# A retention-plus-MLP kernel: the first eight steps written as single operations, in another order on every engine and in the load queue

## The chip, the cores and the metric

One core of one Trainium2 chip runs the whole kernel. The metric is device time in microseconds (us). The kernel before was run nine times: median 701.33 us, 700.83 to 703.13. One of its executions was profiled; that one took 701.53 us by the same clock, and its profile spans 699.7 us, so 1.83 us lie around the span.

## What is computed

```python
# q, k, v: (B, H, S, D) = (4, 8, 768, 64); w_in (512, 2048), w_out (2048, 512); inputs float64
state = zeros((B, H, D, D))
for t in range(S):
    state = gamma * state + k[:, :, t] (outer) v[:, :, t]      # gamma: one number per head
    y[:, :, t] = q[:, :, t] @ state / sqrt(D)
x = y as (B*S, H*D) = (3072, 512)
h = x @ w_in
out = (h - tanh(h)) @ w_out                                    # (3072, 512)
```

q, k and v reach the kernel as float32; w_in and w_out arrive as 64-bit words, and the kernel turns them into float32 itself.

## The kernel before, in words

**Attention.** The 3072 tokens are 24 chunks of 128. For a chunk ci the kernel loads k, q and v (128 x 512 each, `load_chunk`, L230), multiplies q and v by powers of gamma (`scale`, L248), and, for the chunks of the start, turns k and q by four TensorE transposes each (`turn`, L264, matmuls of L276), copied out of PSUM by ScalarE (`turn_copy`, L282). `products` (L314) makes k-v products (L325) and k-q scores (L331). On VectorE `mask` (L335) masks the scores and `state` (L343) adds the chunk to the running state in two operations (L348 or L350, then L354). `outputs` and `outputs_rest` (L379) make y, `see` (L409) is four tiny ScalarE copies on which the second half of the outputs waits, and `keep_x` (L425) copies y into x.

**Weights.** There are 32 weight tiles of 512 KB. Tile W0 to W3 are four column blocks of w_in, W4 to W7 four row blocks of w_out, W8 to W11 columns of w_in again, and so on. A tile of w_in is three DMAs (L159), one of w_out is one (L154). Turning one into float32 is two ScalarE operations (`convert_begin`, L177 and L178), four VectorE operations (`convert_bits`, L186 to L192) and two more, a multiply and an add (`convert_end`, L200 and L204), on GpSimd or VectorE.

**MLP.** A step is 256 tokens by 256 columns of the hidden layer. `up` (L444) makes one half (128 columns) with eight matmul instructions; h lies in one of two PSUM banks. ScalarE then makes u = h*h, tanh(h), two polynomial factors q0 and q1 and the flag `large` (L454 to L472). VectorE does five operations (L482, L486, L495, L502, L503) that end in g. `down` (L511) multiplies g by w_out into the o banks; `add_up` sums o over the runs of steps. Steps 0 and 1 are the first 256 tokens by the first and second 256 columns (weights W0, W1 and W2, W3 going up; W4, W5 and W6, W7 going down), steps 2 and 3 the same for the next 256 tokens, and so on up to step 7. Steps 8 and 9 use W8 to W11 going up.

**Order.** The program is scheduled by hand: every engine runs its instructions in the order of the Python calls, each engine strictly in its own order, and so do the DMAs of the SyncE queue. The order of the first eight steps (`BEGUN = 8`), with chunks 0 to 7 and weights W0 to W11 in them, is a string of pieces, L850 to L859, each a letter and a number. In the kernel before a piece is often several operations:

| piece | what it does | engine |
|---|---|---|
| L, W | load a chunk's k, q, v; load a weight tile | SyncE queue |
| s, w | scale q; scale v | VectorE or GpSimd, by fixed sets (`SCALED`, L806) |
| t, T, c, C | turn k, turn q; copy each out | TensorE; ScalarE |
| p, m, z | products; mask; both state operations | TensorE; VectorE |
| b, e, r, y | outputs, see, rest of the outputs, keep x | TensorE, ScalarE |
| A, D, G | the three parts of a weight's conversion (2, 4 and 2 operations) | ScalarE; VectorE; GpSimd, or VectorE for W0 and W1 (`ENDED`, L807) |
| u, v | the two halves of `up` for a step | TensorE |
| a, q, d, g | u and tanh; three ScalarE factors; first two, last three VectorE operations of a step | ScalarE, VectorE |
| o, E | both `down` products of a step; both sums | TensorE; ScalarE or VectorE |
| x | the next TensorE piece is preceded by so many filler matmuls (`keep_busy`, L215, matmuls of L217, two instructions each) | TensorE |

The filler counts of the kernel before are x8, x4, x5, x3, x3, x5, x7, x2. Buffers that the order has to live with: k and q have two, v four, the raw words of weights three (plus six early places that are later the x tiles), `head`, `low` and `power` two each, q0 and q1 one each, u, tanh, `large` and h two each. After the string a loop runs the other steps (from step 8 on), two steps behind with the `down` products; it begins with W12 and W13, and chunk 8.

Of the kernel before, what the change touches and what calls it, by code (L numbers as in the profile page):

```python
# [16 lines left out]
P = 128  # L17
# [14 lines left out]
def kernel(  # L32
# [137 lines left out]
    def convert_begin(i):  # L170
        if i not in raws:
            return
        raw = raws.pop(i).rearrange("p (n two) -> p two n", two=2)
        lo, hi = raw[:, 0], raw[:, 1]
        head = stage.tile([P, BANK], U32, tag="head", name=f"head_{i}")
        low = stage.tile([P, BANK], F32, tag="low", name=f"low_{i}")
        nc.scalar.activation(head.bitcast(F32), hi.bitcast(F32), AF.Abs)  # L177
        nc.scalar.activation(low, lo, AF.Copy, scale=2.0 ** -52)  # L178
        words[i] = [hi, head, low]

    def convert_bits(i):
        if i not in words:
            return
        hi, head, low = words[i]
        power = stage.tile([P, BANK], U32, tag="power", name=f"power_{i}")
        nc.vector.tensor_scalar(head.bitcast(F32), head.bitcast(F32), HI_MIN, HI_MAX,  # L186
                                op0=ALU.max, op1=ALU.min)
        nc.vector.tensor_scalar(head, head, 3, 0x3FFFFFF8, op0=ALU.logical_shift_left,
                                op1=ALU.bitwise_and)
        nc.vector.scalar_tensor_tensor(head, in0=hi, scalar=0xC0000000, in1=head,  # L190
                                       op0=ALU.bitwise_and, op1=ALU.bitwise_or)
        nc.vector.tensor_scalar(power, head, 0xFF800000, None, op0=ALU.bitwise_and)  # L192
        words[i] = [head, low, power]

    def convert_end(i, engine):
        if i not in words:
            return
        dst, src = weight_ends(i)
        head, low, power = words.pop(i)
        engine.tensor_tensor(low, low, power.bitcast(F32), op=ALU.mult)  # L200
        head = head.bitcast(F32)
        if isinstance(src, list):
            low, head = (t.rearrange("p (c n) -> p c n", c=NC) for t in (low, head))
        engine.tensor_tensor(dst, low, head, op=ALU.add)  # L204

    def convert(i):
        convert_begin(i)
        convert_bits(i)
        convert_end(i, nc.gpsimd)
# [20 lines left out]
    def load_chunk(ci):  # L230
        if ci >= NCH:
            return
        b, j = divmod(ci, CPB)
        loaded[ci] = []
        for nm, src in (("k", k), ("q", q), ("v", v)):
            t = inp.tile([P, H, D], F32, tag=nm, name=f"{nm}_{ci}", bufs=4 if nm == "v" else 2)
            rows = src[b, :, ts(j, P), :]
            if nm == "q" and ci < WIDE:
                for i in range(2):
                    nc.sync.dma_start(  # L240
                        out=t[:, ts(i, RUN)].rearrange("p r d -> p (r d)"),
                        in_=rows[i::2].rearrange("g (p r) d -> p g (r d)", r=RUN),
                    )
            else:
                nc.sync.dma_start(out=t, in_=rows.rearrange("h p d -> p h d"))
            loaded[ci].append(t)

    def scale(ci, which, engine):  # L248
# [4 lines left out]
        if which == 0 and ci < WIDE:  # L253
            if not wide:
                wide.append(mid.tile([P, 2, RUN, 2, D], F32, tag="apart", name="wide", bufs=1))
            out_ = loaded[ci][1] = wide[0][:, ci % 2]
# [7 lines left out]
    def turn(ci, which, early=False):  # L264

        if early:
            tp = bank("o", f"kqTp{which}_{ci}")
        else:
            if which == 0:
                turned[ci] = banks("t", f"kqTp_{ci}")  # L270
            tp = turned[ci][:, which]
# [5 lines left out]
        if early:  # L277
            turned.setdefault(ci, []).append(tp)
# [3 lines left out]
    def turn_copy(ci, which=None):  # L282
        if ci not in sides:
            sides[ci] = mid.tile([P, 2, NP, P], F32, tag="kqT", name=f"kqT_{ci}")
        side = sides[ci]
        for i in range(2) if which is None else (which,):
            tp = turned[ci][:, i] if which is None else turned[ci][i]
            if i:
                nc.scalar.copy(out=side[:, 1].rearrange("p n (t r) -> p n t r", r=RUN),
                               in_=tp.rearrange("p (r t n) -> p n t r", r=RUN, n=NP))  # L290
            else:
                nc.scalar.copy(out=side[:, 0], in_=tp.rearrange("p (n t) -> p n t", n=NP))
# [21 lines left out]
    def products(ci):  # L314

        kh, _, vh = loaded[ci]
# [26 lines left out]
    def state(ci):  # L343
        halves = scores[ci]
        j = ci % CPB
        if j == 0:
            states[ci] = mid.tile([P, 2, NP, D], F32, tag="state", name=f"state_{ci}", bufs=3)
            nc.vector.tensor_copy(states[ci][:, 1], halves[:, 0, 1])  # L348
        else:
            nc.vector.tensor_tensor(states[ci][:, 1], halves[:, 0, 1], states[ci][:, 0],  # L350
                                    op=ALU.add)
        if j < CPB - 1:
# [10 lines left out]
    def outputs(ci):  # L363
# [5 lines left out]
        a_, st = masked.pop(ci), states.pop(ci)  # L369
# [59 lines left out]
    gT = {}  # L429
# [7 lines left out]
    def up(n, m2, i):  # L437

        if (n, m2) not in hps:
            hps[n, m2] = bank("h", f"h_{n}_{m2}")  # L440
        hp = hps[n, m2][:, ts(i, TH)]
        keep_busy(hp[:, :P])
        for c in range(NC):
            nc.tensor.matmul(hp, w1[:, c, ts(2 * m2 + i, P)], xT[n // 2][:, c, ts(n % 2, TH)],  # L444
                             start=(i == 0 and c == 0), stop=(c == NC - 1),
# [358 lines left out]
    EARLY_TURNS = 4  # L804

    SCALED = {2, 4, 5}, {0, 1, 2}  # L806
    ENDED = {0, 1}  # L807

    def engine(i, among):
        return nc.vector if i in among else nc.gpsimd  # L810

    def begin_h(s):

        hps[steps[s][:2]] = bank("h", "h_early")
        keep_busy(hps[steps[s][:2]][:, :P])

    pieces = {
        "L": load_chunk,
        "W": load_weights,
        "s": lambda c: scale(c, 0, engine(c, SCALED[0])),  # L820
        "w": lambda c: scale(c, 1, engine(c, SCALED[1])),
        "t": lambda c: turn(c, 0, c < EARLY_TURNS),
        "T": lambda c: turn(c, 1, c < EARLY_TURNS),
        "c": lambda c: turn_copy(c, 0),
        "C": lambda c: turn_copy(c, 1 if c < EARLY_TURNS else None),
        "p": products,
        "m": mask,
        "z": state,
# [4 lines left out]
        "A": convert_begin,  # L833
        "D": convert_bits,
        "G": lambda i: convert_end(i, engine(i, ENDED)),
        "u": lambda s: up(*steps[s][:2], 0),
        "v": lambda s: up(*steps[s][:2], 1),
        "a": lambda s: shrink_begin(*steps[s][:2]),
        "q": lambda s: shrink_factors(*steps[s][:2]),
        "d": lambda s: shrink_multiply(*steps[s][:2]),  # L840
        "g": lambda s: [f(*steps[s][:2]) for f in (shrink_last_factor, shrink_end)],
        "o": lambda s: [down(*steps[s][:2], j, *steps[s][2:]) for j in range(2)],
        "E": lambda s: [add_up(*steps[s][:2], j) for j in range(2)],
        "h": begin_h,
        "k": lambda s: keep_busy(hps[steps[s][:2]][:, :P]),
# [5 lines left out]
    L0 L1 x8 t0 c0 W0 s0 x4 T0 w0 W1 C0 p0 t1 m0 c1 s1 z0 b0 w1 T1 e0 C1 p1 L2 z1 r0 A0 m1  # L851
    W2 D0 y0 x5 h0 b1 A1 G0 t2 x3 k0 c2 e1 s2 L3 r1 x3 k0 D1 T2 y1 C2 u0 w2 A2 G1 p2 t3 m2 v0 c3 L4 z2
# [205 lines left out]
```

## Time and profile before

| | |
|---|---|
| median of nine runs | 701.33 us |
| the profiled execution | 701.53 us, span 699.7 us |
| busy, share of the span | TensorE 99%, VectorE 74%, ScalarE 62%, GpSimd 51% |
| first eight steps on TensorE, by the timeline | from the first transposes at 4.63 us to the end of step 5's down products at 91.90 us |
| VectorE busy from 0 to 92 us | 70.45 us |
| DMA over the first 58 us | 12.6 MB by the SyncE queue |

Times within the profile count from the start of the span. A row of the timeline reads: start, length, engine, line, operation, output <- input, shape, count, and in brackets the idle time ahead of it with what ended it. A row of the chain of waits reads: start, length, engine and line that the end of the program can be followed back to. "PE" is TensorE's matmuls, DVE is VectorE, ACT is ScalarE, POOL is GpSimd, SP is SyncE.

### The profile page before, as it was taken

To read this page: it belongs to the slowest core of one execution; us is meant where nothing else is said; L and a number is where in the kernel's file an instruction comes from. 1 tells how busy PE (TensorE), PEld (TensorE's weight loads), DVE (VectorE), ACT (ScalarE), POOL (GpSimd) and SP (SyncE) were. 2 spreads that over 40 slices of the span, in tenths; PEclk is the share of its full clock that TensorE was granted. 3 is DMA by queue.
4 is the path that set the end of the run, shared out by engine and by line. 5 is a ranking of instruction groups with operands and counts; after the bars stand their busy time and mean duration, and the time that the engine had idled before them with its cause. 6 is when DMAs were issued, how large, how long until landed. Compare 5 with 4: busy or idle time off the path is not lost.

```text
span 699.7 us, 16645 instructions
## 1 busy us (share of the span) xinstructions
PE 691.7 (99%) x6602; PEld 580.5 (83%) x6602; DVE 519.8 (74%) x888; ACT 432.6 (62%) x818; POOL 356.2 (51%) x523
## 2 busy tenths in 40 slices
PE   8999999999999999999999999999999999999997
PEld 7786666676767667789999999999999999999996
DVE  4898889989898865677776686677686676766765
ACT  4577677676866755565555665555665555566553
POOL 1364445554454686878854453354443444544333
PEclk9999999999999999999999999999999999999999
DMA  8790439978778666500000000000000000000001
GB/s 228 212 276 24 135 107 218 214 202 223 190 210 212 180 166 171 161 34 2 0 1 16 16 1 30 2 1 31 2 1 31 1 1 31 0 17 16 1 16 47
DMA packets 119678, 59.97 MB, mean 86 GB/s; under 512 B 101808, under 2 KB 112688, under 8 KB 119600
## 3 DMA queue, kind: packets, MB, share of 16 engines
q1 hardware_dynamic: 117008, 50.21, 28.1%
q10 hardware_dynamic: 2592, 8.69, 3.3%
q8 instruction: 52, 0.85, 0.5%
q14 instruction: 26, 0.21, 0.1%
HBM read 35.83 MB, written 14.68 MB: 72 GB/s over the span
## 4 chain that ended last, share of the span: by engine, by line
PE 92%; DVE 3%; DMA 2%; ACT 1%; issue 1%; POOL 0%; POOLq 0%; DVEq 0%; ACTq 0%
PE h L758 28%; PE o L511 15%; PE h L444 14%; PE fast_t L649 10%; PE y L649 8%; PE fast_o L649 8%; PE y L379 3%; PE s L331 2%; PE s L325 1%; PE kqTp L276 1%; DMA kqT<-rows 1%; PE h_early L444 1%; DMA rows<-apart 1%; PE kqTp L217 1%; PE h_early L217 1%
## 5 line engine op out<-in xcount | busy, mean ns | idle before, releaser
L600 POOL TENSOR_TENSOR s<-g 128x128 f32<-128x128 f32 x64 | 29.3, 458 | 190.5 <-DVE g L503 186.6
L457 ACT ACTIVATE th<-h 128x512 f32<-128x512 f32 x64 | 38.2, 598 | 142.4 <-DVE h L775 139.9
L511 PE MATMUL o<-w,g 128*128 128x512 f32 x256 | 115.9, 595 | 0.0
L444 PE MATMUL h<-xT,w 128*128 128x256 f32 x480 | 110.2, 382 | 0.0
L444 PEld LDWEIGHTS h<-xT,w 128*128 128x128 f32 x480 | 90.1, 190 | 20.6 <-issue 8.9
L503 DVE COPY_PREDICATED g<-large,th 128x512 f32<-128x512 int32 x96 | 81.7, 851 | 9.7
L511 PEld LDWEIGHTS o<-w,g 128*128 128x128 f32 x256 | 47.6, 190 | 47.4 <-issue 44.5
L758 PEld LDWEIGHTS h<-xT,w 128*128 128x128 f32 x512 | 76.8, 191 | 8.4 <-ACT fast_head L763 1.0
L482 DVE TENSOR_TENSOR th<-h,th 128x512 f32<-128x512 f32 x94 | 64.2, 683 | 21.3 <-ACT th L455 20.0
L773 DVE TENSOR_TENSOR h<-h,fast_head 128x256 f32<-128x256 f32 x64 | 27.7, 432 | 68.7 <-PE h L758 63.3
L758 PE MATMUL h<-xT,w 128*128 128x128 f32 x512 | 78.3, 275 | 0.2 <-ACT fast_head L763 0.2
L200 POOL TENSOR_TENSOR low<-low,power 128x512 f32<-128x512 f32 x30 | 39.6, 1321 | 63.1 <-DVE power L192 53.6
L495 DVE SCALAR_TENSOR_TENSOR g<-q,h 128x512 f32<-128x512 f32 x64 | 44.0, 688 | 36.1 <-ACT q L471 34.8
L463 ACT ACTIVATE q<-u,tab 128x512 f32<-128x512 f32 x96 | 69.7, 726 | 1.8
L471 ACT ACTIVATE q<-u,tab 128x512 f32<-128x512 f32 x96 | 69.5, 723 | 0.0
L472 ACT ACTIVATE large<-u,tab 128x512 f32<-128x512 f32 x96 | 68.5, 713 | 0.0
L758 PE MATMUL h<-x,w 128*128 128x128 f32 x448 | 68.3, 275 | 0.0
L486 DVE SCALAR_TENSOR_TENSOR h<-q,h 128x512 f32<-128x512 f32 x94 | 64.9, 691 | 3.7 <-ACT q L463 3.7
L758 PEld LDWEIGHTS h<-x,w 128*128 128x128 f32 x448 | 59.0, 192 | 0.0
L763 ACT COPY fast_head<-h 128x512 f32<-128x512 f32 x64 | 37.5, 585 | 19.2 <-PE h L758 19.1
L502 DVE TENSOR_TENSOR g<-g,u 128x512 f32<-128x512 f32 x64 | 47.5, 742 | 0.0
L768 POOL TENSOR_TENSOR fast_head<-fast_head 128x256 f32<-128x256 f32 x64 | 46.9, 732 | 1.0 <-ACT fast_head L763 1.0
(195 smaller groups left out, 1487.8 us busy)
## 6 DMA issues: line engine op xcount, KB each, us to landing
rows<-apart ACTq DMA_DIRECT2D x16, 512.0 KB, 4.4
k<-in_k_dram SPq DMA_DIRECT2D x24, 256.0 KB, 3.8
v<-in_v_dram SPq DMA_DIRECT2D x24, 256.0 KB, 5.2
raw<-in_moe_w_out_dram SPq DMA_DIRECT2D x12, 512.0 KB, 4.2
out_dram<-sum SPq DMA_DIRECT2D x22, 256.0 KB, 2.0
q<-in_q_dram SPq DMA_DIRECT2D x16, 256.0 KB, 4.8
raw<-in_moe_w_in_dram SPq DMA_DIRECT2D x14, 256.0 KB, 4.3
raw<-in_moe_w_in_dram SPq DMA_DIRECT2D x28, 128.0 KB, 4.3
```

The lines of the kernel that those rows point to most:

```text
L444: nc.tensor.matmul(hp, w1[:, c, ts(2 * m2 + i, P)], xT[n // 2][:, c, ts(n % 2, TH)], start=(i == 0 and c == 0), stop=(c == NC - 1), skip_g ...
L463: nc.scalar.activation(q0, shrinking[n, m2][0], AF.Square, bias=bias0)
L471: nc.scalar.activation(q1, u, AF.Square, bias=bias1, scale=math.sqrt(A))
L472: nc.scalar.activation(large, u, AF.Relu, bias=bias_m)
L482: nc.vector.tensor_tensor(th, hp, th, op=ALU.subtract)
L486: nc.vector.scalar_tensor_tensor(hp, in0=shrinking[n, m2][2], scalar=C0, in1=hp, op0=ALU.add, op1=ALU.mult)
L502: nc.vector.tensor_tensor(flat, src, u, op=ALU.mult)
L503: nc.vector.copy_predicated(flat, large.bitcast(I32), th)
L511: nc.tensor.matmul(o_p[j], gT[n, m2][:, i, ts(j, P)], w2[:, 2 * m2 + i], start=(first and i == 0), stop=(last and i == 1))
L649: nc.tensor.matmul(accs[n][k], left[k - 1], right, start=first and k in (1, 6, 7, 4), stop=last, skip_group_check=True)
L758: nc.tensor.matmul(hps[n, m2][:, ts(PLACE[k], P)], s_of[m2][k - 1][:, c], x_of[n][k - 1][:, c], start=(k == 1 and c == 0), stop=(c == 1), ...
L768: nc.gpsimd.tensor_tensor(odd_room[1], first[:, :2], first[:, 3:1:-1], op=ALU.add)
```

## The change

The functions are cut into single operations. `load_one` loads k, q or v alone. `convert_begin` becomes `convert_head` (A) and `convert_low` (l); `convert_bits` can do any of its four operations alone (D1 to D4); `convert_end` gives its multiply to `convert_low_end` (F) and keeps the add (G). The two state operations are z and Z. The five ScalarE operations of a step are au, ath, aq0, aq1, alarge, and the five of VectorE f0 to f4; `down` and `add_up` have a piece per half (o0, o1, E0, E1). The pieces s, w, F and G take their engine from the order: D is VectorE, P is GpSimd. The `SCALED` and `ENDED` sets are gone, and so is `begin_h`. The loop from step 8 on is not changed. Its core, and the new order in full:

```diff
-    def load_chunk(ci):
+    def load_one(ci, which):
...
+    def convert_low_end(i, engine):
+        if i not in words:
+            return
+        low, power = (words[i][x] for x in ("low", "power"))
+        engine.tensor_tensor(low, low, power.bitcast(F32), op=ALU.mult)
...
             if not wide:
-                wide.append(mid.tile([P, 2, RUN, 2, D], F32, tag="apart", name="wide", bufs=1))
-            out_ = loaded[ci][1] = wide[0][:, ci % 2]
+                room = mid.tile([P, 2, RUN, 2, D], F32, tag="apart", name="wide", bufs=1)
+                wide.extend([room[:, i % 2] for i in range(WIDE)])
+            out_ = loaded[ci][1] = wide.pop()
...
-        if (n, m2) not in hps:
+        begins = (n, m2) not in hps
+        if begins:
             hps[n, m2] = bank("h", f"h_{n}_{m2}")
...
-                             start=(i == 0 and c == 0), stop=(c == NC - 1),
+                             start=(begins and c == 0), stop=(c == NC - 1),
...
+    def activate(s, x):
+        hp, u = hps.get(steps[s][:2]), early.get((s, "u"))
+        out_ = early[s, x] = work(x, 1 if x[0] == "q" else 2)
...
+    def multiply(s, i):
...
-        "G": lambda i: convert_end(i, engine(i, ENDED)),
+        **{f"D{i + 1}": lambda c, i=i: convert_bits(c, (i,)) for i in range(4)},
+        "F": convert_low_end,
+        "G": convert_end,
...
     order = """
-    L0 L1 x8 t0 c0 W0 s0 x4 T0 w0 W1 C0 p0 t1 m0 c1 s1 z0 b0 w1 T1 e0 C1 p1 L2 z1 r0 A0 m1
-    W2 D0 y0 x5 h0 b1 A1 G0 t2 x3 k0 c2 e1 s2 L3 r1 x3 k0 D1 T2 y1 C2 u0 w2 A2 G1 p2 t3 m2 v0 c3 L4 z2
...
+    Lk:0 Lq:0 Lv:0 x:9 t:0 s:0D Lq:1 x:3 T:0 W:0 w:0D Lk:1 c:0 C:0 A:0 x:2 p:0 z:0 Lv:1 m:0
+    Z:0 s:1P Lq:2 D1:0 D2:0 w:1D T:1 b:0 Lk:2 Lv:2 t:1 C:1 l:0 e:0 c:1 D3:0 r:0 x:2 p:1 W:1
+    D4:0 y:0 t:2 c:2 z:1 s:2P T:2 Lk:3 w:2P C:2 m:1 Z:1 b:1 p:2 e:1 r:1 F:0D A:1 G:0D D1:1 y:1
+    D2:1 z:2 Lq:3 Lv:3 Z:2 D3:1 l:1 W:2 s:3P x:1 t:3 w:3P u:0 m:2 Lq:4 c:3 T:3 s:4P C:3 D4:1
+    b:2 p:3 F:1D e:2 r:2 l:2 A:2 G:1D v:0 z:3 m:3 D1:2 y:2 Lv:5 Z:3 au:0 Lk:4 D2:2 D3:2 t:4
+    Lv:4 T:4 Lq:5 b:3 Lk:5 w:4P w:5D W:3 c:4 D4:2 F:2D C:4 e:3 W:4 W:5 ath:0 r:3 y:3 aq0:0
+    aq1:0 p:4 f0:0 z:4 m:4 Z:4 l:3 f1:0 A:3 alarge:0 u:2 G:2P t:5 s:5P T:5 v:2 D1:3 b:4 D2:3
+    D3:3 D4:3 A:4 c:5 F:3P f2:0 C:5 l:5 ath:2 Lq:6 Lk:6 Lv:6 W:7 e:4 G:3P Lq:7 W:8 W:9 p:5
+    au:2 Lv:7 r:4 aq0:2 y:4 A:5 aq1:2 l:4 f3:0 u:1 f0:2 m:5 z:5 f4:0 s:6P t:6 W:6 w:6P T:6
+    Lk:7 W:10 v:1 W:11 s:7P b:5 f1:2 f2:2 f3:2 c:6 C:6 au:1 p:6 e:5 D1:5 D1:4 D2:5 D2:4 r:5
+    D3:5 aq1:1 alarge:2 alarge:1 aq0:1 ath:1 u:3 D3:4 D4:5 v:3 D4:4 F:5P z:6 m:6 F:4D Z:6 f0:1
+    G:4D au:3 T:7 G:5P t:7 f1:1 A:6 y:5 c:7 f2:1 D1:6 o1:0 f4:2 w:7P C:7 b:6 D2:6 f3:1 p:7
+    aq0:3 e:6 ath:3 r:6 l:6 v:4 u:4 D3:6 m:7 f0:3 f1:3 D4:6 z:7 F:6P G:6P y:6 l:7 alarge:3
+    aq1:3 f2:3 f3:3 A:7 D1:7 b:7 f4:1 o0:0 A:11 e:7 D2:7 D3:7 D4:7 F:7P G:7D u:5 r:7 v:5 o1:1
+    o0:1 ath:4 au:4 aq0:4 l:11 f0:4 f4:3 f1:4 l:9 aq1:4 f2:4 f3:4 D1:11 E1:1 alarge:4 A:9 D1:9
+    D2:9 D2:11 D3:9 E0:1 y:7 ath:5 au:5 aq0:5 aq1:5 alarge:5 o1:2 v:7 D3:11 D4:11 o0:2 o1:3
+    D4:9 u:7 F:9D G:9P f0:5 o0:3 f1:5 F:11D f2:5 f3:5 f4:4 f4:5 G:11P A:8 D1:8 D2:8 E1:3 D3:8
+    Z:7 au:7 l:8 A:10 D1:10 D4:8 l:10 aq1:7 D2:10 F:8D D3:10 ath:7 f0:7 aq0:7 E0:3 D4:10 u:6
+    v:6 o0:4 au:6 o1:4 F:10P f1:7 f2:7 ath:6 alarge:7 G:10P f0:6 aq1:6 aq0:6 f1:6 alarge:6
+    o0:5 o1:5 E0:5 f3:7 f2:6 Lv:8 f3:6 f4:7 f4:6 Lk:8 Lq:8 W:12 W:14 W:13 G:8P E1:5
     """
     for piece in order.split():
-        pieces[piece[0]](int(piece[1:]))
+        kind, at_ = piece.split(":")
+        if at_[-1] in engines:
+            pieces[kind](int(at_[:-1]), engines[at_[-1]])
+        else:
+            pieces[kind](int(at_))
```

Per engine it reads so. TensorE: `t0 T0 p0 T1 b0 t1 r0 p1 t2 T2 b1 p2 r1 t3 u0 T3 b2 p3 r2 v0 t4 T4 b3 r3 p4 u2 ...`, with fillers x9, x3, x2, x2, x1. The loads: `k0 q0 v0 q1 W0 k1 v1 q2 k2 v2 W1 k3 q3 v3 W2 q4 v5 k4 v4 q5 k5 W3 W4 W5 q6 k6 v6 W7 q7 W8 W9 v7 W6 k7 W10 W11 v8 k8 q8 W12 W14 W13`. On VectorE the operations that move there from GpSimd are s0, w5, F2, G7, F4, G4, F9, F11 and F8; from VectorE to GpSimd go s2, w2, s4 and s5.

## The prediction

> **What bounds the kernel now.** The page first: which engine is full, and how full the DMA is over time.
>
> ```profile
> PE 691.7 (99%) x6602; PEld 580.5 (83%) x6602; DVE 519.8 (74%) x888; ACT 432.6 (62%) x818; POOL 356.2 (51%) x523
> PE   8999999999999999999999999999999999999997
> DMA  8790439978778666500000000000000000000001
> ```
>
> TensorE is the bound over the whole span, so time can only come out of what TensorE does or misses early. But fillers (L217) count as busy. So the chain of waits second, for stretches that are not work:
>
> ```profile
> 28.22 1.31 PE h_early L217 x10
> 29.53 0.86 PE y L379 x48
> 30.39 1.02 PE kqTp L276 x8
> 31.41 1.56 PE h_early L217 x14
> ...
> 85.19 6.87 PE o L511 x16
> 92.06 3.45 PE h L444 x16
> ```
>
> Fillers stand on the chain itself. The timeline prices real work from start to start: a chunk's two turns 0.93 us (43.70 to 44.63), products 0.94 (47.26 to 48.20), outputs 0.75 (46.51 to 47.26), rest 0.39 (43.31 to 43.70), so 3.0 a chunk and 24.1 for eight. An up half takes 1.73 to 1.92, 28.8 for sixteen at 1.8; the down products of a step take 3.44 (71.26 to 78.12 for two), 20.6 for six. That is 73.5 us. TensorE takes from 4.63 to 91.90 us for it, 87.3: **13.8 us** are filler (about 7.6, from the L217 rows after 4.63) or waiting (6.2). That is all this change can win.
>
> Third, the busy time of each engine in stretches, to see what is full next:
>
> ```profile
> 10.00:92.00 82.00, 80.04 (x1207) 59.59 (x1204) 68.32 (x118) 55.00 (x130) 37.57 (x30) 1.00 0.57 160
> 92.00:140.00 48.00, 47.86 (x453) 32.63 (x452) 44.58 (x67) 35.92 (x61) 25.21 (x20) 1.00 0.84 197
> ```
>
> The columns after the stretch are its length and TensorE's matmul, weight-load, VectorE, ScalarE and GpSimd busy time, clock, DMA share, GB/s. VectorE is at 0.833 in the first steps and 0.929 right after: it is the next bound.
>
> **The loads, the first term.** In the 2 us windows from 2 to 16 us the queue moves 260 GB/s on average (233 to 297), so it is full. A tile lands at about 2 us + (bytes up to and with it) / 0.26 MB per us + 1.6 us: q1 (1.31 MB) by this at 8.6, seen 8.37; W0 (2.1 MB) at 11.7, seen 12.05. From 34 to 48 us the windows show 294 GB/s. In the new order k1 comes at 1.83 MB (it now stands behind W0), 10.6 us; W1 at 3.4 MB, 16.7; k3 17.7; k4 24.9; v4 25.9; W3 29.8; k7 at 11.5 MB, about 46.
>
> **TensorE up to t7, the second term.** I walk each engine's list with the row durations; an operation starts when its own engine, its inputs and its buffers are free. Before, after:
>
> - p0: 8.0, 8.0. s0 on VectorE takes 0.69 where GpSimd took 1.04, but x9 for x8 fillers gives it back.
> - t1: 8.63, 10.6 (k1). Then p1: 11.05, 12.7, since v1's scaling on VectorE stands behind the first two bit operations of W0. So far a **loss** of 1.7 us, and TensorE idles about a microsecond.
> - t2 and T2: 15.03 and 18.30, 13.7 and 14.4. q2 lands at 12.7 and its 1.04 us on GpSimd wait for nothing; before it stood on VectorE behind W0's eight operations. p2: 20.89, 15.8 (v2, landed 14.7, 1.04 on GpSimd).
> - u0: 18.76, 18.3. It wants y1, and y1 stands on ScalarE behind A1, which waits for W1 (16.7).
> - t3: 21.98, 17.7. p3: 27.11, 21.6 (C3 stands behind y1 and l1). v0: 22.84, 22.9.
> - p4: 33.98, 27.5. Here the x5 of h2, the x7 and the x2 are gone (3.5 us); x1, at t3, is all that is left.
> - u1: 41.39, 35.2. It wants step 0's bank, so f3:0, which VectorE ends at 34.8. p6: 47.26, 40.7.
> - t7: 53.13, **46.7**. T7 and t7 are 0.5 us each here; k7 has landed at 46.
>
> **From t7 to the end, the third term.** What is left is the same on both sides: eight up halves, all down products, and one chunk's remains. Before it takes 91.90 - 53.13 = 38.8 us with no filler in it, so the shift at t7, 6.4 us, is what the change gives if nothing waits afterwards. But VectorE is what the rest waits for. Its work: 70.45 us busy before 92; four scalings go to GpSimd and two come (-1.4), seven multiplies or adds of weights come at 0.69 each (+4.8): **73.9**. Some 2.1 of it lie before 10 us. At 0.93 (what 92 to 140 shows) 71.8 us end at 87.2. Walking it: o1:0 waits 0.9 for G4 on VectorE (47.6); v4 wants f3:1 at 51.6, when TensorE is there at 51.6; G7 waits 1.3 for F7 on GpSimd and comes 0.4 before o1:1; u6 has 2 us to spare. Step 8 wants W8: F8 lies 8.1 us of VectorE work before its end, and three GpSimd operations behind it (F10, G10, G8, 3 x 1.28) bring G8 to about 84.3, ahead of TensorE. So one wait of 0.9, and places with 0 to 0.4 us of cover. For those I take another 0.6, between none and the 3.3 us by which VectorE rows before are longer than their like.
>
> ```profile
> 16.86 0.69 DVE L204 TENSOR_TENSOR w<-low,head 128x512 f32<-128x512 f32 x1
> ...
> 21.38 1.42 DVE L204 TENSOR_TENSOR w<-low,head 128x512 f32<-128x512 f32 x1
> ```
>
> ```profile
> 21.14 1.11 POOL L262 TENSOR_TENSOR wide<-q,tab 128x512 f32<-128x512 f32 x1 [11.72 <-DMA q<-in_q_dram]
> 22.21 1.49 POOL L262 TENSOR_TENSOR v<-v,tab 128x512 f32<-128x512 f32 x1
> ```
>
> Both adds are alike; the second had GpSimd reading beside it. The others are 40.32 (1.15 for 0.43), 47.36 (1.80 for 0.74) and 56.04 (1.56).
>
> The Trainium skill, "SBUF — State Buffer", section "Who interferes with whom", has this: VectorE with two inputs in SBUF and GpSimd reading SBUF use one port pair, and whoever issues second waits for the whole instruction. Moving work from GpSimd to VectorE makes fewer meetings, but VectorE is now full, so a meeting costs TensorE time; by the rule alone, were all seven moved operations hit as L204 was, 7 x 0.73 = 5.1 us would go. The rows show four hits in 92 us.
>
> The other edge costed at nothing is the missing fillers. The first sixteen filler instructions take 3.79 us, 0.237 each; the ten at 28.22 take 0.131. So TensorE starts at about half speed and is full by 5.7 us; after that its idle gaps reach 0.69 us without a slower row behind them, and the new ones about 1 us. If the speed fell again from 11 to 22 us, the 8 us of work there would double; 3 us of that hide in the waits for loads, so this edge costs between 0 and 5 us. I take 0, by the gaps seen. The skill's "TensorE: Matmul & The Clock Gate", "Part 1: The HAM clock gate", speaks against dropping fillers: an idle window of about 3.4 us brings the clock back to half. By it gaps of 1 us are safe; no row here shows a longer one.
>
> **The sum.** 6.4 - 0.9 - 0.6 = 4.9 us: TensorE ends step 5 at 87.0 for 91.90. The loop behind is unchanged and TensorE-bound (47.86 of 48 us), so the shift stays: 701.53 - 4.9 = **696.6 us**. The profiled execution lies 0.20 above the median of the nine, within their spread. W14 and W13 now wait in the load queue for W10's third bit operation (about 80 us), land by 87, and ScalarE wants W13 at 89: covered by 2 us; if not, the wait is the difference.
>
> **Rivals.**
>
> 1. *The loads are late (no change).* k7 stands behind W7, W8, W9 and W6. For: the 12.6 MB before took until 56 us, with 0.69 to 0.39 of DMA share from 20 to 26 us. If the queue is as slow now, the last two tiles behind k7 (1.05 MB, 3.6 us) put it at 52.4, and t7 is 5.7 us late: 6.4 - 5.7 leaves 0.7, **700.8**. Against: those low shares came from waits for buffers (k4 on p2, and so on), which now are free sooner.
> 2. *VectorE becomes the bound (slower).* Place: F8 on VectorE, behind it GpSimd's F10, G10, G8, and step 8. Price: at a share s VectorE ends at 10 + 71.8/s. At 0.833, as before, that is 96.2; F8 ends 9.7 earlier, D4:10 is 2.2 on, three GpSimd operations take 3.8: 92.5, 0.6 late, and with step 6's down products 0.8: 702.3. At 0.80 it ends at 99.8, step 8 begins at 95.8 and the down products wait too: +4.4, **706**. It decides from about 0.84 down. For: the tight places above, each a chain ScalarE, VectorE, GpSimd in which one late link is handed round. Against: 0.929 is seen right behind.
> 3. *No slip at all.* Without the 1.5 us of waits, and without the 0.8 that the walk has ahead of t7 at t4 (k4, 0.3) and r3 (the see copies, 0.5), 7.2 us: **694.3**.
> 4. *The early order gives nothing* and only the later fillers go (3.5 us): 698.0; it lies in the forecast's spread.
>
> **How the numbers follow.** Forecast, 694.3 to 699.8: 70%. No slip or better: 6%. Loads late, 699.8 to 701.5: 10%. VectorE the bound: 14%, most of it over 702.4. A measurement of this kernel tells 0.2% (1.4 us) from no change: under 699.9 is faster. Faster 0.77 (0.70 + 0.06 + a little of the loads), same 0.09, slower 0.14. The range goes from 694.3 to 702.4, the price of VectorE at its present share; 6% lie below, some 12% above.
>
> **What would show it.** Right: t1 after 10 us and p1 later than 11.05, but p3 by 23 and t7 by 48 us; L217 rows of only 34 instructions; step 5's down products ending between 85 and 89; VectorE at 0.9 or more from 25 us on. Wrong: transposes of chunk 7 waiting for the k load; TensorE waiting for L204 or L502 on VectorE after 47 us; h rows at twice 0.22 us before 25 us; ScalarE waiting for W13.

## The result, and the profile after

The changed kernel takes **699.13 us** (median of ten runs, 698.35 to 700.11) where the kernel before, run beside it, took 701.62 (30 runs, 700.83 to 703.13): a ratio of **0.9964 [0.9956, 0.9972]**, some 2.5 us faster. The forecast was 4.9 us. Its profiled execution took 697.04 us (span 695.3), 4.5 us less than the one of before, so the trace that is read here is 2.1 us faster than the median of its own kernel, while that of before stood at its median. What a median run does differently from the trace is half of what there is to explain. Three single runs among all those told of here (one of `new_old_engines`, two of the kernel before) took twice the time, 1441.56 to 1452.76 us, and are left out everywhere.

The page of the changed kernel, first busy times, then TensorE, its clock and the DMA in 40 slices of the span:

```profile
PE 685.1 (99%) x6562; PEld 575.2 (83%) x6562; DVE 517.6 (74%) x893; ACT 433.2 (62%) x818; POOL 349.7 (50%) x518
PE   8999999999999999999999999999999999999997
PEclk9999999999999999999999999999999999999999
DMA  8991268878878567400000000000000000000001
```

TensorE is busy for 6.6 us less: its 40 instructions less are all fillers. The DMA is fuller in the second slice (9 for 7). The stretches that stood at 80.04 and 47.86 us of TensorE:

```profile
10.00:92.00 82.00, 77.58 (x1160) 57.21 (x1150) 69.61 (x127) 59.22 (x138) 32.80 (x27) 1.00 0.58 162
92.00:140.00 48.00, 48.00 (x452) 32.43 (x451) 45.48 (x69) 35.92 (x66) 25.19 (x21) 1.00 0.84 218
```

From 92 to 140 us TensorE has no gap. From 10 to 92 us it has 4.4 us of gaps, more than the 2.0 of before, and yet it is done sooner, since most of the fillers are gone. The chain of waits, which went through fillers before, now goes through a load:

```profile
43.70 5.49 DMA k<-in_k_dram
49.19 0.04 issue
49.23 0.66 PE kqTp L297 x4
...
81.07 6.87 PE o L530 x16
87.94 3.45 PE h L463 x16
```

Step 5's down products end at 87.77 by the timeline (91.90 before): 4.1 us. What lies behind is the same on both sides: the span ends 607.5 us later here and 607.8 before. So in both of these executions the time is decided by the place where step 5 ends. The starts of the main pieces, in us (the last column is another profiled execution of the changed kernel, told of below):

| | before | predicted | after | after, again |
|---|---|---|---|---|
| t1 | 8.63 | 10.6 | 10.58 | 12.56 |
| p1 | 11.05 | 12.7 | 13.18 | 15.37 |
| t2 | 15.03 | 13.7 | 14.52 | 17.28 |
| p2 | 20.89 | 15.8 | 16.92 | 19.79 |
| u0 | 18.76 | 18.3 | 19.57 | 22.59 |
| p3 | 27.11 | 21.6 | 22.67 | 25.70 |
| p4 | 33.98 | 27.5 | 29.62 | 32.58 |
| p6 | 47.26 | 40.7 | 42.85 | 47.24 |
| t7 | 53.13 | 46.7 | 49.23 | 54.59 |
| step 5's end | 91.90 | 87.0 | 87.77 | 93.13 |
| from t7 to that end | 38.8 | 40.3 | 38.5 | 38.5 |

The timeline of TensorE has few waits (the bracket ends a row: idle time, and what ended it); the ones for the load of k, at both ends of the stretch, and the largest between:

```profile
10.58 0.63 PE L297 MATMUL kqTp<-tab,k 128*128 128x128 f32 x4 [0.44 <-DMA k<-in_k_dram]
...
29.62 0.69 PE L342 MATMUL s<-v,k 64*64 64x64 f32 x32 [0.70 <-POOL v L281]
...
49.23 0.66 PE L297 MATMUL kqTp<-tab,k 128*128 128x128 f32 x4 [0.86 <-DMA k<-in_k_dram]
```

After 49.23 no row has such a bracket: TensorE waits for nothing that lasts 0.2 us. The filler line has 34 instructions, as the string says (its rows: tiles, count, then minimum, median and maximum in ns, then first and last start):

```profile
L232 PE MATMUL kqTp<-w x26: 275/421/583, 1.1 to 18.6; 128*128 128x128 f32 x26
L232 PE MATMUL s<-w x8: 275/275/377, 6.8 to 12.5; 128*128 128x128 f32 x8
```

### The profile page after: what moved, and what is told of

Its sections match the earlier page's. It is cut to its first block, busy times and chain, and to the rows that moved or that the text cites. A ratio compares the mean times of both kernels' runs of the same rounds, so it can differ in the third digit from the quotient of the medians.

```text
span 695.3 us, 16551 instructions
## 1 busy us (share of the span) xinstructions
PE 685.1 (99%) x6562; PEld 575.2 (83%) x6562; DVE 517.6 (74%) x893; ACT 433.2 (62%) x818; POOL 349.7 (50%) x518
## 4 chain that ended last, share of the span: by engine, by line
PE 93%; DMA 2%; DVE 2%; SPq 1%; issue 1%; ACT 1%; POOL 0%; POOLq 0%; DVEq 0%; ACTq 0%
PE h L777 28%; PE o L530 16%; PE h L463 16%; PE fast_t L668 10%; PE y L668 8%; PE fast_o L668 8%; PE y L397 3%; PE s L342 1%; DMA k<-in_k_dram 1%; PE s L348 1%; DMA raw<-in_moe_w_in_dram 1%; PE kqTp L297 1%; SPq L159 0%; SPq L254 0%; SPq L259 0%
## 5 line engine op out<-in xcount | busy, mean ns | idle before, releaser
L463 PE MATMUL h<-xT,w 128*128 128x256 f32 x512 | 118.0, 382 | 0.3 <-ACT xT L443 0.3
L463 PEld LDWEIGHTS h<-xT,w 128*128 128x128 f32 x512 | 96.0, 190 | 22.7 <-issue 9.3
L777 PEld LDWEIGHTS h<-xT,w 128*128 128x128 f32 x512 | 76.8, 191 | 8.4 <-ACT fast_head L782 1.0
L522 DVE COPY_PREDICATED g<-large,th 128x512 f32<-128x512 int32 x88 | 74.0, 841 | 9.0
L501 DVE TENSOR_TENSOR th<-h,th 128x512 f32<-128x512 f32 x88 | 60.0, 682 | 20.4 <-ACT th L474 19.2
L482 ACT ACTIVATE q<-u,tab 128x512 f32<-128x512 f32 x88 | 63.8, 725 | 1.7
L490 ACT ACTIVATE q<-u,tab 128x512 f32<-128x512 f32 x88 | 63.6, 723 | 0.0
L505 DVE SCALAR_TENSOR_TENSOR h<-q,h 128x512 f32<-128x512 f32 x88 | 60.7, 690 | 2.6 <-ACT q L482 2.6
L491 ACT ACTIVATE large<-u,tab 128x512 f32<-128x512 f32 x88 | 62.6, 712 | 0.0
L208 POOL TENSOR_TENSOR low<-low,power 128x512 f32<-128x512 f32 x25 | 33.0, 1318 | 55.7 <-DVE power L201 46.7
```

The lines of the kernel that those rows point to most:

```text
L482: nc.scalar.activation(q0, shrinking[n, m2][0], AF.Square, bias=bias0)
L490: nc.scalar.activation(q1, u, AF.Square, bias=bias1, scale=math.sqrt(A))
L491: nc.scalar.activation(large, u, AF.Relu, bias=bias_m)
L501: nc.vector.tensor_tensor(th, hp, th, op=ALU.subtract)
L505: nc.vector.scalar_tensor_tensor(hp, in0=shrinking[n, m2][2], scalar=C0, in1=hp, op0=ALU.add, op1=ALU.mult)
L522: nc.vector.copy_predicated(flat, large.bitcast(I32), th)
```

## Experiments

The theory to begin with: TensorE's time is set by where chunk 7's turn stands, the tail behind it is constant, and the changed kernel's median is slower than its trace because its waits ahead of that place (loads above all) differ from one execution to the next. The main rivals: VectorE is the bound in other executions; the missing fillers cost time after all.

**The changed kernel once more, `again_after`.** No edit.

> The changed kernel again, nothing altered. Open: its profiled execution took 697.04 us, its ten timed ones 699.13 in the median (698.35 to 700.11). Theory A (executions differ in when loads land: the wait of chunk 7's transposes for k, 0.86 us in the first profile, is longer in most): time 699.1, and this second profile, if it is a slower one, shows 1 to 3 us at that wait or at other waits for loads before 50 us, and from there to the end of step 5's down products 38.5 us again. Theory B (VectorE is the bound in most executions): the extra lies after chunk 7's transposes, so that stretch takes 39.5 us or more. Theory C (the profiled execution is always faster than the timed ones): again about 697 for it and 699 for the others.

Median 700.2 us (698.46 to 702.39, nine runs), ratio 0.9967 [0.9956, 0.9978]. The profiled execution is the slowest of the nine, 702.39. Of TensorE's rows, the two with the longest waits, and between them two whose wait nothing in the profile ends ("issue"):

```profile
12.56 1.09 PE L297 MATMUL kqTp<-tab,k 128*128 128x128 f32 x4 [2.00 <-DMA k<-in_k_dram]
...
21.39 0.45 PE L397 MATMUL y<-a,v 64*64 64x64 f32 x12 [0.38 <-issue]
...
27.30 0.40 PE L348 MATMUL s<-kqT 64*64 64x64 f32 x13 [0.72 <-issue]
...
54.59 0.65 PE L297 MATMUL kqTp<-tab,k 128*128 128x128 f32 x4 [1.91 <-DMA k<-in_k_dram]
```

Stretches around the first one (length, busy times of the five engines, clock, DMA share, GB/s):

```profile
11.00:12.00 1.00, 0.00 (x0) 0.00 (x0) 0.43 (x1) 1.00 (x3) 0.00 (x0) 1.00 0.61 157
12.00:13.00 1.00, 0.44 (x2) 0.47 (x3) 0.43 (x1) 0.88 (x6) 0.00 (x0) 0.50 0.69 177
...
18.00:19.00 1.00, 1.00 (x6) 0.85 (x4) 1.00 (x3) 0.51 (x1) 0.00 (x0) 0.58 1.12 264
19.00:20.00 1.00, 1.00 (x66) 0.96 (x68) 0.96 (x2) 0.66 (x2) 0.00 (x0) 1.00 0.79 201
```

The first theory holds for this execution. From t7 to the end it is 38.5 us here too; t7 itself is 5.4 us later. k1 lands 2 us later, TensorE stands still for 2 us, its granted clock falls to 0.50 from 12 to 18.8 us (the four turns of t1 take 1.09 us instead of 0.63). Between p4 and p6 waits of 0.70 and 0.50 us for ScalarE's copies bring 1.4 us more, and at k7 TensorE waits for 1.91 us instead of 0.86. VectorE is not the bound in this one either: it is busy for 55.91 of the 67 us from 25 to 92, a share of 0.83.

**k7 earlier in the queue, `k7_early`.**

```diff
 # load queue
 ... Lk:6 Lv:6 W:7 Lq:7
+Lk:7
 W:8 W:9 Lv:7 W:6
-Lk:7
 W:10 W:11 ...
```

> The changed kernel with one load moved: k of chunk 7 stands right behind q of chunk 7, ahead of W8, W9, v of chunk 7 and W6. Theory A: the wait of chunk 7's transposes for k (0.86 us in the profile) goes, TensorE is ahead by that from there on; if the timed executions lose more there, the time falls by up to 2 us: 697 to 698.3. Theory B (VectorE, or a load other than this one, is the bound): the wait moves to the next operation and the time stays at 699.1, within 0.5 us.

700.63 us (699.19 to 700.91), ratio 0.9966 [0.9953, 0.9978]: no gain. Chunk 7 no longer waits for k; other waits take its place, on TensorE

```profile
19.19 0.45 PE L397 MATMUL y<-a,v 64*64 64x64 f32 x12 [1.60 <-issue]
...
39.14 0.69 PE L342 MATMUL s<-v,k 64*64 64x64 f32 x32 [1.70 <-ACT kqT L306]
```

and, behind the second, on ScalarE:

```profile
37.46 0.67 ACT L175 ACTIVATE head<-raws 128x512 f32<-128x512 f32 x1 [1.21 <-DMA raws<-in_moe_w_out_dram]
38.03 0.58 ACT L309 COPY kqT<-kqTp 128x512 f32<-128x512 f32 x1
```

The copies that p5 wants stand on ScalarE behind A4, which waits for W4: a load once more, through a third engine. After each of the two stops the clock is at 0.50 for 3.4 us (from 20.0 and from 40.5), and t7 is at 53.05.

**The old order of the load queue, all else new, `new_old_loads`.**

```diff
 # load queue
-k0 q0 v0 q1 W0 k1 v1 q2 k2 v2 W1 k3 q3 v3 W2 q4 v5 k4 v4 q5 k5 W3 W4 W5 ...
+k0 q0 v0 k1 q1 v1 W0 W1 k2 q2 v2 W2 k3 q3 v3 k4 q4 v4 W3 k5 q5 v5 W4 W5 ...
```

> The changed kernel with the load queue in the order of the kernel before (k1, q1, v1 ahead of W0; W1 ahead of k2; W6 and W7 and chunk 7 in their old places), all else as changed. Theory L (the load order is needed for the gain): products of chunk 1 come at 11.3 us again, but chunk 2 and 3's transposes wait for W1 and land 1 to 2 us later than in the changed kernel (t3 at 19.5 or later for 18.71), chunk 7's k is early; about 700, plus or minus 1. Theory E (the order on the engines makes the gain, loads don't matter): 699.1 within 0.6, or a little faster because chunk 7's k is early.

702.05 us (700.58 to 704.11, 11 runs), ratio **0.9997 [0.9988, 1.0006]**: the whole gain is gone. The largest wait is in chunk 0:

```profile
15.68 0.70 PE L397 MATMUL y<-a,v 64*64 64x64 f32 x16 [3.36 <-ACT seen L427]
```

The see copies of chunk 0 stand behind A0 on ScalarE, and A0 waits until 13.6 us for W0, which is now behind k1, q1, v1. Behind this stop the clock is at 0.50 from 15.4 to 22.2 us, and all eleven runs have a mean granted clock of 0.994 to 0.997, so half clock is part of the loss. The new load order is worth the whole gain *to this order of the engines*; what it would be worth with the old engine order isn't shown by this.

**Before, without its later fillers, `old_no_late_fill`.** The kernel before with six pieces of filler taken out of the string:

```diff
-W2 D0 y0 x5 h0 ... t2 x3 k0 ... r1 x3 k0 ... A3 x5 h2 ... T4 x7 k2 r3 x2 k2 ...
+W2 D0 y0 h0 ... t2 k0 ... r1 k0 ... A3 h2 ... T4 k2 r3 k2 ...
```

> The kernel before with its fillers x8 and x4 kept and the other six sets (x5, x3, x3, x5, x7, x2: 50 instructions, 6.6 us on TensorE) left out; they compute nothing. Theory F (fillers stood in the way, mostly those from 28 us on, 3.5 us, and the order does little): the time falls by 2.5 to 3.5 us, to about 698.5, as much as the whole change brings. Theory W (fillers filled waits that stay): less than 1 us. Theory G (without them TensorE's clock falls and its rows get longer): h rows at more than 0.24 us each before 40 us, no gain or slower.

702.62 us (700.98 to 707.11, 12 runs), ratio **1.0022 [1.0003, 1.0041]**. Fifty filler instructions less, and the kernel is not faster but a little slower. The stops are there, and the work behind them is slow:

```profile
15.25 1.13 PE L379 MATMUL y<-kqT,state 64*64 64x64 f32 x32 [2.23 <-ACT xT L425]
...
35.79 0.70 PE L379 MATMUL y<-a,v 64*64 64x64 f32 x16 [2.62 <-ACT seen L409]
...
38.85 3.78 PE L444 MATMUL h_early<-xT,w 128*128 128x256 f32 x8
```

An up half of 1.73 to 1.99 us takes 3.78, and the clock from 38 to 42 us is 0.50. Each run has its mean granted clock over the span: one of the twelve has 0.999, and takes 700.98; the five at 0.990 to 0.992 take 705.55 to 707.11. The kernel before, in 87 runs beside these experiments, never had less than 0.999. A mean of 0.990 over 705 us is 7 us of full-speed time missing; part of it hides in waits. Even the one run with the clock up wins only 1.3 us on the 702.25 of the kernel before in this set, where 6.6 us of filler were taken out.

**More fillers, and fewer, in the new order: `new_more_fill`, `new_no_fill`.**

```diff
 # TensorE, new_more_fill
-... b:0 t:1 r:0 x:2 p:1 t:2 T:2 b:1 p:2 ...
+... b:0 x:4 t:1 r:0 x:4 p:1 t:2 T:2 b:1 x:2 p:2 ...
 # TensorE, new_no_fill
-x:9 t:0 x:3 T:0 x:2 p:0 T:1 b:0 t:1 r:0 x:2 p:1 ... r:1 x:1 t:3 ...
+x:9 t:0 T:0 p:0 T:1 b:0 t:1 r:0 p:1 ... r:1 t:3 ...
```

> The changed kernel with ten more filler instruction pairs where TensorE waits anyway: x4 ahead of chunk 1's k transposes, x4 for x2 ahead of its products, x2 ahead of chunk 2's products; they compute nothing. In the second profile of the changed kernel TensorE stood still for 2.0 us there and its granted clock was 0.50 from 12 to 18 us; in the first it stood for 0.4 and the clock stayed 1.00. Theory G (the clock falls when TensorE stands still long enough, and that costs 1 to 3 us in the executions where it happens): the clock is 1.00 in all 1 us windows from 6 to 40 us, the granted clock of every run 0.999 or more, and the median 0.5 to 1.5 us lower than the changed kernel's against the same kernel before, with less spread. Theory D (the lateness is all that matters, the clock costs nothing since TensorE waits for loads anyway): no gain, or 0.3 us slower for the fillers in the way.

> The changed kernel with only the nine fillers at the start: x3, x2, x2, x1 (16 instructions) are left out; they compute nothing. Theory G: with longer stretches without work between 5 and 14 us more runs show a granted clock of 0.995 or less, and the median is 0.5 to 2 us slower than the changed kernel. Theory D: TensorE waits for loads there anyway, so 0 to 0.5 us faster.

With more (eight pairs by the edit, 16 instructions): 699.35 us (697.94 to 700.05, six runs), 0.9963 [0.9951, 0.9976], every run at a clock of 0.999 or more. With none but the first nine: 699.78 (697.86 to 703.09, 12 runs), 0.9975 [0.9962, 0.9988], nine of the twelve runs at 0.998 or less. The intervals overlap: fillers steady the clock here too, but are not worth a difference that can be told. In the profile of `new_no_fill` the clock falls at 12.6 us, after two stops of less than 1 us each (the row of 1.13 us is at half clock), and doesn't fall after a stop of 2.16 us:

```profile
11.05 0.63 PE L297 MATMUL kqTp<-tab,k 128*128 128x128 f32 x4 [0.94 <-DMA k<-in_k_dram]
...
12.33 0.53 PE L397 MATMUL y<-a,v 64*64 64x64 f32 x16 [0.65 <-ACT seen L427]
...
13.24 1.13 PE L342 MATMUL s<-v,k 64*64 64x64 f32 x32 [0.38 <-DVE v L281]
...
20.83 0.69 PE L297 MATMUL kqTp<-tab,k 128*128 128x128 f32 x4 [2.16 <-DMA k<-in_k_dram]
```

**The old engines, all else new, `new_old_engines`.**

```diff
-s:0D w:5D F:2D F:4D G:4D G:7D F:9D F:11D F:8D  s:2P w:2P s:4P s:5P
+s:0P w:5P F:2P F:4P G:4P G:7P F:9P F:11P F:8P  s:2D w:2D s:4D s:5D
```

> The changed kernel in its new order and with its new load queue, but the thirteen operations that changed engine are back where they were (s0, w5, F2, F4, G4, G7, F8, F9, F11 on GpSimd; s2, s4, s5, w2 on VectorE). Theory P (the prediction's: q2's scaling off VectorE brings chunk 2 forward, and GpSimd at 1.28 us an operation would hold g's weights): chunk 2's q transposes at 15.5 us or later for 14.98, step 0's first down product 1 to 2 us later, 700 to 701.5. Theory O (order and loads make the gain, the engine is all one): within 0.6 us of the changed kernel.

701.61 us (699.66 to 703.72, 11 runs), ratio **0.9999 [0.9988, 1.001]**: here, too, the whole gain is gone. The profiled execution is the fastest of them:

```profile
15.85 0.63 PE L297 MATMUL kqTp<-tab,wide 128*128 128x128 f32 x4 [0.65 <-DVE wide L281]
...
20.70 0.45 PE L397 MATMUL y<-a,v 64*64 64x64 f32 x12 [2.04 <-issue]
```

The first is the predicted reason (q2's scaling behind weight 0's operations on VectorE), at 0.65 us. The second has no releaser at all, and is the largest; more on it at the end. In this execution the clock is at 1.00 and t7 at 51.54. Nine of the other ten runs have a mean clock of 0.998, so the profile doesn't show what a usual run of this kernel loses.

**A better start? `early_fix`, `early_fix_a4`.** Three loads (k1, q1, v1) go ahead of W0 and k7 forward; on ScalarE chunk 0's see copies, chunk 1's copies and x go ahead of A0, on VectorE chunk 1's operations ahead of D0; the second kernel also puts A4 behind the copies of chunk 5.

```diff
 # load queue
-k0 q0 v0 q1 W0 k1 v1 q2 ... q7 W8 W9 v7 W6 k7 W10 ...
+k0 q0 v0 k1 q1 v1 W0 q2 ... q7 k7 W8 W9 v7 W6 W10 ...
 # TensorE
-p:0 T:1 b:0 t:1 r:0
+p:0 t:1 T:1 b:0 r:0
 # ScalarE
-c:0 C:0 A:0 C:1 l:0 e:0 c:1 y:0
+c:0 C:0 c:1 C:1 e:0 y:0 A:0 l:0
 # VectorE
-D1:0 D2:0 w:1D D3:0 D4:0 z:1 m:1 Z:1
+w:1D z:1 m:1 Z:1 D1:0 D2:0 D3:0 D4:0
 # ScalarE, early_fix_a4 alone
-A:4 c:5 C:5
+c:5 C:5 A:4
```

> The changed kernel with k1, q1, v1 ahead of W0 in the load queue and k7 behind q7; and, so that W0's later landing holds nothing up, ScalarE takes W0's two operations behind the copies of chunk 0 and 1, VectorE scales v1 first and does W0's four bit operations behind chunk 1's state, and TensorE turns k1 ahead of q1. W1, W2 and the rest as in the changed kernel. Theory A (the waits for k1 and k7, and the clock that falls behind the first, are what keeps most executions from the 697 us of the first profile): chunk 1's k transposes at about 8.7 us without a wait, products at 12.5, no wait at k7, clock 1.00 throughout, 697 to 698.3 against 699.1 of the changed kernel. Theory B (W1's landing at about 17 sets the first up product and what follows, whatever comes before): within 0.5 us of the changed kernel.

> As early_fix, and ScalarE takes W4's first operation behind the copies of chunk 5 instead of ahead of them. In the profile of early_fix it stood 1.02 us waiting for W4 there, and TensorE's products of chunk 5 waited 1.00 us for the copies behind it (1.70, 1.48 and 1.37 in other profiles). Theory S (strict order on ScalarE makes one late load hold up work that doesn't need it): that wait goes, chunk 5's products come by 36.7 for 37.71, and the median is 0.5 to 1 us below early_fix's 699.3, 698.3 to 698.8, ratio to before 0.9950. Theory B (loads as a whole set chunk 7): the wait moves to a later load (k, q or v of chunk 6 or 7) and the time stays within 0.4 us of early_fix.

699.3 us (698.29 to 699.64, five runs), 0.9962 [0.995, 0.9975], and 700.01 (697.57 to 701.94, 12 runs), 0.9968 [0.9956, 0.998]: neither can be told from the changed kernel. Both take away the wait that they aim at, and get others. Of `early_fix`, beside a stop of 1.11 us without a releaser:

```profile
37.71 0.69 PE L342 MATMUL s<-v,k 64*64 64x64 f32 x32 [1.00 <-ACT kqT L306]
```

and of `early_fix_a4`, where the second is gone:

```profile
23.21 0.66 PE L297 MATMUL kqTp<-tab,wide 128*128 128x128 f32 x4 [1.72 <-POOL wide L281]
```

**The wait without a releaser: `w1_late`, `w1_late_k7`.** W1 goes behind v3 in the queue (the second kernel also moves k7 as above, and has the first two fillers of `new_more_fill`), so that the queue is emptier at 15 us. These two leave out part of the computation: three of W1's four VectorE bit operations stand ahead of its A in the string and do nothing, some 1.5 us of VectorE work less.

```diff
 # load queue
-... q2 k2 v2 W1 k3 q3 v3 W2 ...
+... q2 k2 v2 k3 q3 v3 W1 W2 ...
 # ScalarE, VectorE
-e:1 A:1 y:1 l:1 c:3 C:3 ... G:0D D1:1 D2:1 z:2 Z:2 D3:1 m:2 D4:1
+e:1 y:1 c:3 A:1 C:3 l:1 ... G:0D z:2 Z:2 m:2 D1:1 D2:1 D3:1 D4:1
```

> The changed kernel with W1 behind chunk 3's loads instead of ahead of them (the queue then waits for chunk 1's products before k3, so little is in flight just after 14 us); ScalarE takes W1's first operation behind y1 and c3, VectorE W1's bit operations behind chunk 2's state and mask. Open: in the profiles of seven kernels with the new order, TensorE stands still inside the outputs_rest of chunk 1 or nearby for 0 to 2.0 us with no releaser shown, always at the same instruction, and in each it goes on 2.3 to 2.6 us after a 16 KB transfer of the instruction queue (that transfer is at 15.5 us in the first profile, where nothing waits, and at 16.8 to 18.9 in the others). Theory K (TensorE waits for its code, whose transfer is held up by the loads that are queued ahead of it): with the queue nearly empty after 14.3 us the 16 KB transfer comes by 15.5, no wait inside chunk 1's outputs_rest; chunk 0's first up product, freed of W1, starts by 19 us; 697.5 to 698.8, against 699.1 to 699.3 of the changed kernel. Theory D (that stop has nothing to do with the loads): it stays, between 0.4 and 2 us. Theory B (loads as a whole set the time of chunk 7's transposes): the early times move and the total stays within 0.4 us of the changed kernel.

> As w1_late, with chunk 7's k right behind its q in the load queue and with x4 fillers ahead of chunk 1's transposes and products (x4 for x2 there); the fillers compute nothing. If theories A, G and K each hold for their part (k7's wait, the clock's fall behind k1, the code's wait), the three add up: 697 to 698.3 and a granted clock of 0.999 or more in every run. If theory B holds (loads as a whole): within 0.4 us of w1_late.

702.35 us (700.15 to 704.76, 12 runs), 1.0008 [0.9993, 1.0022], and 702.47 (700.34 to 703.47, 11 runs), 1.0008 [0.9999, 1.0017]: slower than the changed kernel. The wait stays in the first:

```profile
18.67 0.45 PE L397 MATMUL y<-a,v 64*64 64x64 f32 x12 [0.98 <-issue]
```

The theory was that TensorE waits there for its own code, held up behind the loads. The last 16 KB transfer of the instruction queue ahead of that row starts at 16.4 us, where the theory wanted it by 15.5; in the second it starts at 15.5 and there is no wait. So an emptier load queue alone doesn't do it. The mean clock parts the runs again: in the first, the six at 0.997 to 0.999 take 700.15 to 702.04, the two at 0.989 take 704.39 and 704.76.

**The kernel before once more, `old_again`.**

> The kernel before once more, for a second profile of it. Theory K says its fillers and its other order keep TensorE behind the code: no wait of more than 0.5 us without a releaser, granted clock 1.00 in all windows, step 5's down products ending at 91.5 to 93 us. If it shows such waits, its typical execution has them as well and they cancel in the comparison.

701.33 us. From t7 (53.13) to step 5's end (91.90) its marks are those of the first profile within 0.01 us, though p2 to p4 differ by 0.2 to 0.25 us, and there is no wait without a releaser over 0.2 us. In the changed kernel t7 was at 49.2 in one profile and at 54.6 in the other.

## Why the prediction was right, and only by half

**What held.**

- *"TensorE is the bound ... so the shift stays."* Shown: the remainder behind step 5 is 607.8 us before, 607.5 after, and 607.5 in `again_after`.
- *"From t7 to the end: what is left is the same on both sides."* Shown, and better than forecast: 38.8 us before; 38.5 in both profiles of the changed kernel.
- *The loads first, a loss at the start, then the gain.* t1 was forecast at 10.6 and came at 10.58; p1 at 12.7, came at 13.18, a loss of 2.1 us to before; p2 has won 4.0, p3 4.4. Chunk 7 waits for k7, but by 0.86 us and not by 5.7 (first rival).
- *VectorE is not the bound* (against the second rival). It is busy for 72.51 us up to 92, forecast 73.9, and from 25 to 92 us for 57.25 of 67, a share of 0.85; the sign asked for 0.9. TensorE, with no wait after 49.23, did not feel it from there on. Of the meetings with GpSimd that the prediction weighed, VectorE's timeline shows three rows that are long for their kind, each beside a GpSimd row; two of them are

```profile
13.76 1.15 DVE L201 TENSOR_SCALAR power<-head 128x512 uint32<-128x512 uint32 x1
...
16.10 1.31 DVE L208 TENSOR_TENSOR low<-low,power 128x512 f32<-128x512 f32 x1
```

The third starts at 91.61 (L194, 1.37 us for 0.42). Together they are 2.3 us longer than their like, where the four long rows of before made 3.3. The other multiplies and adds of weights on VectorE up to 92 us take 0.69 to 0.83. The 5.1 us that the rule of the Trainium skill's page "SBUF — State Buffer", "Who interferes with whom", would have given at its worst are not there.

**What failed.**

- *Two signs.* Transposes of chunk 7 waiting for k were named as a sign of being wrong, and they do wait. Of the signs of being right, t7 by 48 us (it came at 49.23) and VectorE at 0.9 did not come; t1, p1, p3, the 34 fillers and step 5's end did.
- *The slip of 0.9 + 0.6 us behind t7* did not come. The 0.9 was o1:0 waiting for G4; G4 ends at 48.95, and k7 holds TensorE to 49.23 anyway. The margin for late links was not needed.
- *The walk to t7* was 2.5 us too early (46.7, came 49.23), and that in the better profile: 0.5 late at p1 (0.51 for the see copies, 0.36 for v1's scaling), 1.1 at p2 (0.48 for v2's), 2.1 at p4 (0.64 for see copies, 0.70 for v4's scaling on GpSimd, which starts at 28.52 where v4 was to land at 25.9), 2.5 at t7 with k7. The two errors, -2.5 and +1.8, nearly cancel: 87.77 for 87.0, 697.04 for 696.6. That the one trace fits so well is luck.
- *"I take 0" for the missing fillers*, judged by the gaps of one trace. The trace after has no gap that counts (its clock is 1.00 throughout), which makes the step look right; `again_after` has a gap of 2.0 us and 6.8 us at half clock. Of 20 executions of the changed kernel four have a mean clock of 0.996 or less, so this moves its median little and its upper end more. `old_no_late_fill` shows what fillers are for: taking 25 of the 37 from the old order wins nothing, and in the worst runs loses 5 us. So the 7.6 us of filler among the "13.8 us" that "this change can win" were not simply there to be won. Nor is the other part, 6.2 us called waiting, all idle time: it is what the priced work leaves over, while TensorE's busy time up to 92 us (88.38) leaves 3.6 us idle, 1.05 of them at the very start. The Trainium skill's "TensorE: Matmul & The Clock Gate", "Part 1: The HAM clock gate", was read as making gaps under some 3.4 us safe; here the clock fell after single waits from 1.60 us up and after two of 0.94 and 0.65 us, and the measurement decides.
- *A time from one execution.* The prediction took each load's landing as one number. The two profiles of before agree at t7 to the hundredth, which seems to allow that; but the 30 runs of before spread over 2.3 us, no less than the ten of the changed kernel (1.8), so two profiles don't show that order to be steady. The new order runs close behind its loads, and in `again_after` what k1 and k7 were late by went into t7. This is the term that was mis-sized most. Worked back from the median: 699.13 less the 1.8 around the span, less 607.5, less 38.5 puts t7 of a median run at 51.3, 2.1 us behind the profiled one and 1.8 ahead of the 53.13 of before: the sum's shift of 6.4 us at t7 is 3.9 in the trace and 1.8 by this working. (In `new_more_fill`, profiled in an execution of 700.05 us at a clock of 1.00, t7 is at 52.13 and the same 38.5 and 607.5 us follow.) A t7 of 51.3 lies nearer to the first rival's 52.4 than to the forecast's 46.7: by this working the median is inside the forecast's spread, 694.3 to 699.8, only because the 1.5 us of slip behind t7 stayed away. That these 2.1 us are loads and stops without a releaser, as in `again_after`, is likely, for in most of these runs the clock is at 0.999 or more; but runs without a profile show no waits, so it is not shown.

**Where the gain comes from** can't be split. Undoing the load order alone gives back everything (0.9997), undoing the engine moves alone also (0.9999). The first does so through A0, which stands ahead of work that does not need W0, and through the half clock behind that stop. How the second does so is not shown: the waits of 0.3 to 0.7 us and the stop without a releaser stand in its fastest execution, which lost little. And no wait that was taken away (k7's, k1's, p5's) made the kernel measurably faster: another one, of 1.0 to 1.7 us, came in its place. None of the versions tried beats the changed kernel by more than the measurement can tell.

## What to carry to other kernels

In a stretch that waits for loads as much as for the busiest engine, one profile of an order says little: walk the order twice, with each load landing once early and once 2 us late, and forecast between the two. Before counting fillers as time to win, look at the gaps that would be left: gaps that added up to some 1.6 us within one beat of 3.4 us (told of below) brought 3.4 or 6.8 us at half clock here. Moving one late load forward in a full queue moved the wait here, not the end.

## What the runs showed of the hardware

- **The granted clock changes on a beat of 3.41 us, and the length of one stop alone does not decide whether it falls.** It went to 0.50 after TensorE had stood for 1.60 and 1.70 us (`k7_early`), 1.72 (`early_fix_a4`), 2.00 (`again_after`), 2.23 and 2.62 (`old_no_late_fill`), 2.19 (`new_no_fill`) and 3.36 us (`new_old_loads`), and after 0.94 and 0.65 us close together (`new_no_fill`); not after 2.04 in `new_old_engines`, 2.16 in `new_no_fill`, 1.91 in `again_after` or 1.50 in `new_old_loads`. In windows of 0.1 us the times at which it changes lie, within a trace, whole multiples of 3.41 us apart: 20.0, 23.4, 40.5 and 43.9 in `k7_early`, 12.6, 16.0, 53.5 and 56.9 in `new_no_fill`; each fall lasts one or two such beats. If the beats are laid over the six traces that have a fall, TensorE stood idle for 1.59 to 3.10 of the 3.41 us in all nine beats at whose end the clock fell; from 4 to 62 us no other beat at full clock has more than 1.50, but for one of 1.63 (`again_after`, 52.96 to 56.37). So the border here is some 1.6 us of idle time within a beat, in one stop or in several. The 2.16 us of `new_no_fill` lay across two beats, with 0.75 and 1.42 us idle in them. For the 2.04 us of `new_old_engines` this can't be tried, since a trace without a change of clock doesn't show its beats.
- **TensorE stops behind a transfer of the instruction queue.** A stop with no releaser ("issue") comes in five profiles at the fifth matmul of chunk 1's second outputs: 0.38 us (`again_after`), 1.60 (`k7_early`), 2.04 (`new_old_engines`), 1.11 (`early_fix`) and 0.98 (`w1_late`). In each of these a transfer of the instruction queue (16 KB) begins 2.3 to 2.5 us before TensorE goes on: at 18.9 for 21.39, 16.8 for 19.19, 18.3 for 20.70, 17.2 for 19.57 and 16.4 for 18.67, in the same order. In the profile after it begins at 15.5 and nothing waits; the two profiles of before have no such stop. In `new_more_fill`, with 16 filler matmuls more ahead of it, the stop comes 16 matmuls earlier (18.71, 0.25 us), so its place goes by the count of TensorE's instructions. A second one follows 126 matmuls later in `again_after` (27.30, 0.72 us, the next transfer at 24.8). All this fits TensorE waiting for its own code; no run alters the code's transfer alone, so it is not shown. What sets the moment at which the transfer starts is open: in `w1_late` an emptier load queue didn't bring it forward to 15.5.
